# A 640-point inverse transform regrouped by residues modulo 5, with accumulating DMAs for one of its parts

## The chip, the cores and the metric

The kernel runs on one core of one Trainium2 chip. The metric is the time of one execution on the device in microseconds. A core has TensorE (PE, with its weight loads as PEld), VectorE (DVE), ScalarE (ACT), GpSimd (POOL) and SyncE (SP); each runs its own instruction queue in order. SP and POOL also issue DMAs, which 16 DMA engines carry out.

## The reference, cut to what matters

```python
xn = layernorm(x)                                   # x: 2048 x 640, bf16
X  = rfft2(xn)                                      # 2048 x 321 complex
s  = irfft2(X * (w_r + 1j * w_i)).astype(bfloat16)  # 2048 x 640
g  = silu((gelu(xn @ w_gate) * (xn @ w_up)) @ w_down)   # inner width 1536
return x + s * g
```

There are two branches, a spectral filter and a gated feed-forward network. They meet in the last line.

## The kernel before, in words

The 2048 rows are 16 slabs of 128 rows: slab n1 holds the rows that are n1 modulo 16. Four slabs make a group g of the feed-forward branch.

**Order of the work.** Everything is laid out by hand. The list `back` has 144 entries, called slots here; each slot is a piece of the feed-forward branch, and `plan[s]` holds the items of the spectral branch that `put` hangs behind slot s. The program goes through the slots in order and emits a slot's piece, then its items. Every engine sees its own instructions in that order. TensorE's queue is therefore fixed, and an engine that is late holds up whatever stands behind it in its own queue.

**Feed-forward branch.** `ffn_half(g, t, k)` is one slot: five matmuls of 128x512 into a bank `psg` (k=0, gate) or `psu` (k=1, up), both at L809. ScalarE applies gelu to psg (L814), and VectorE multiplies it by psu into `UT` (L816). The pool `psA` has two banks of each tag, so each tag has one bank ahead. Slots 96 to 107 are the down projection of group 2 and slots 108 to 131 are the 24 halves of group 3. The down projection of groups 1 and 2 is made by `product`, seven block products in place of eight for two slabs at a time: six matmuls of 320 columns each (L903), sums of its left operands by `u_sum` on VectorE (L884), and additions out of PSUM on VectorE (L910). Where the sum is complete, ScalarE takes a tanh (`th`, L847) and VectorE finishes the gate (L852), one and two products later, through `flush`. `down_third` does it directly: 12 matmuls per half slab (L946), and ScalarE applies silu to the bank (L844). In group 3, the last, slabs 12 and 13 go through `product` (slots 132 to 137) and slabs 14 and 15 through `down_third` (slots 138 to 143).

**Spectral branch.** The forward stages end with the array `B2`. From slot 67 on eleven bursts (`s2_in`, `s2_out`) do the filter: 4 to 5 matmuls into `px` (L649), ScalarE copies px to `xs` (L657), VectorE multiplies xs with the two filter tables into `RZ` (L661), and one burst later TensorE multiplies into `pu` (L674). ScalarE copies pu to `RX` (L681), the even and the odd columns apart, and SP writes RX to DRAM (`UDR`, L684). `load_V` reads it back with rows and columns exchanged (L699) into `VY` (slabs 0 to 3) and `W` (slabs 4 to 15).

The inverse transform follows, slab by slab:

- `gather` copies the columns that fill a fifth block of 128 into `vr` (VectorE, L709). Its tile has two buffers.
- `slab_S1i`, the transform over rows: five matmuls of 128x128 into `pv` (L730), one for each 128-column block of V as the weights. ScalarE copies pv to a slab of `vs` (L732).
- `group_Di`, the 640-point transform over columns, for up to three slabs at once through `d_group`: 12 matmuls of 160 columns with 128 rows (L573) and 12 with 32 rows (L577) into two tiles `pd`. ScalarE copies and scales them into `eobuf` (L755).
- `group_cs` and `group_Y`: VectorE adds and subtracts even and odd parts (L761), then writes the two halves of a row of Y, one of them backwards (L770, L772).
- `finish`: VectorE multiplies Y by the gate (L788). For slabs 0 to 11 (`XA = 12`) POOL issues a DMA that adds x out of DRAM to Y in place (L790); for the others VectorE adds x (L792). SP then writes the slab out (L793).

px, pu, pv and pd all come from the pool `psB`, which has two buffers: the third of a row of such tiles waits until the first has been copied out.

Slot 98 is called `vs0`. A group of three slabs starts every seven slots from there: S1i at +1, +2 and +4, D at +6, cs at +7 and +8, Y at +9 and +10, finish at +11 to +13.

Of the kernel before, what the change touches and what calls it, by code (L numbers as in the profile page):

```python
# [14 lines left out]
P = 128  # L15
# [61 lines left out]
def build(nc, env):  # L77
# [71 lines left out]
    FI = consts.tile([P, 5, LH], BF16)  # L149
# [91 lines left out]
    lint = gtile([LH], INT32)  # L241
    nc.gpsimd.iota(lint, pattern=[[1, LH]], base=0, channel_multiplier=0)
# [10 lines left out]
    ftm = gtile([5, LH], FP32)  # L253
# [49 lines left out]
    kc = []  # L303

    def fwd_consts():
        cq = affine("cq", h_f, -320.0, 320.0)
# [4 lines left out]
        kc.append(cq)  # L311
        ab.extend([(a_m, b_0), (a_m, b_1), (a_m, b_2), (a_m, b_3), (a_y, None)])
# [3 lines left out]
    def inv_consts(part):  # L316
        if part == 0:
            for k, c in enumerate((0.0, 4.0, 2.0)):
                inv_src[k] = affine(f"i_{k}", pf, 4.0, c)
            kc.append(affine("hk", h_f, -2.0, 1.0))  # L320
        else:
            o = [affine(f"o_{k}", pf, 2.0, c) for k, c in enumerate((320.0, 2.0, 321.0, 1.0))]
            i_0, i_1, i_2 = (inv_src[k] for k in range(3))
            ab.extend([(i_0, o[0]), (i_1, o[1]), (i_2, o[2]), (i_2, o[3])])

    def inv_rest():
        cq, hk = kc
        l_s, l_k, l_r, i_r, o_r = (c1(n) for n in ("l_s", "l_k", "l_r", "i_r", "o_r"))
        for out, in0, s1, s2 in ((l_s, s_f, 2.0, 256.0), (l_k, h_f, 2.0, l_s), (l_r, hk, hi_f, l_k),
                                 (i_r, l_r, 2.0, 0.0), (o_r, l_r, 1.0, cq)):  # L330
            nc.gpsimd.tensor_scalar(out=out, in0=in0, scalar1=s1, scalar2=s2, op0=ALU.mult, op1=ALU.add)
        ab.append((i_r, o_r))
# [28 lines left out]
    fv = gtile([10, LH], FP32)  # L361

    def ft_v(g):
        if g < 5:
            parts = [(0, TW, meo[:, g // 2])] if g < 4 else [(0, 66, mys), (66, TW, mys)]
        else:
            parts = [(0, LH, lint)]
# [4 lines left out]
    FW = (TW, LH)  # L372
# [194 lines left out]
    def d_group(lhs, T, w):  # L567
        ps = [psB.tile([P, 2, 512], FP32, tag="b", name=f"pd{b}") for b in range(2)]
        n = len(lhs)
        out = [[ps[g // 2][:, g % 2, a * w:(a + 1) * w] for g in range(4)] for a in range(n)]  # L570
        for a in range(n):
            for g in range(4):
                nc.tensor.matmul(out[a][g], lhsT=lhs[a][:, g, :], rhs=T[:, g, 0:w], start=(a == 0), stop=False)  # L573
        for a in range(n):
            for g in range(4):
                r = slice(32 * g, 32 * g + 32)
                nc.tensor.matmul(out[a][g], lhsT=lhs[a][r, 4, :], rhs=T[r, 4, 0:w], start=False, stop=(a == n - 1))  # L577
        return [t[:, :, 0:n * w].rearrange("p k (a m) -> p a k m", a=n) for t in ps]

# [50 lines left out]
    WB = LH + 1  # L630
    BURSTS = [(h0, 3, l0, w) for h0 in range(0, 15, 3) for l0, w in ((0, WB), (WB, L - WB))]
# [8 lines left out]
    def s2_in(b):  # L640
# [3 lines left out]
        for lo in range(2):  # L644
            r = slice(64 * lo, 64 * lo + 64)
            for hh in range(2):
                for i, j, kind in s2_tiles(b, lo, hh):
# [3 lines left out]
                                     stop=(j == n))  # L651

# [11 lines left out]
    def s2_out(b):  # L664
# [25 lines left out]
    VO = (0, L + 1, LH, L + 1 + HD)  # L690
# [13 lines left out]
    def gather(i):  # L704
# [3 lines left out]
        for k, c0, w in ((0, 0, LH), (1, L + 1, HD)):  # L708
# [453 lines left out]
```

## Time and profile before

| | |
|---|---|
| median of 3 runs | 196.37 us (195.82 to 196.56) |
| profiled execution | 197.07 us |
| its span | 195.2 us |
| granted TensorE clock | 1.0 |
| TensorE busy | 187.4 us, 96% |
| VectorE busy | 154.5 us, 79% |
| ScalarE busy | 126.6 us, 65% |
| POOL busy | 50.5 us, 26% |

All rows of the profile come from one execution, of 197.07 us; 1.9 us of it lie outside the span. Busy shares are means over stages: by stretches of the span, TensorE is busy for 9.55 of the 10 us from 124 to 134 and 10.98 of the 11 us from 134 to 145, and VectorE for 9.55 of those 11. A busy time of an instruction includes its start-up, which overlaps the instruction before it: a row of VectorE additions of 0.48 us each starts every 0.40 us. In a line of the timeline the idle time before the instruction and what ended it stand in brackets.

### The profile page before, as it was taken

Reading aid. Unit: us, or ns where it says so; the run is one execution under the profiler, and the core shown is the slowest. Engines: PE = TensorE matmul, PEld = TensorE weight load, DVE = VectorE, ACT = ScalarE, POOL = GpSimd, SP = SyncE. Lnnn points to the kernel's source line nnn. Section 1 sums busy time; section 2 is a strip of 40 time slices with the busy share of each in tenths; the row PEclk is TensorE's granted clock in tenths of the full one; section 3 lists DMA queues with packets and bytes.
Section 4 is the critical chain, followed back from the end, with each engine's and each line's share of the span. In section 5 each row is a group of like instructions: output and inputs, shape, how many; then the busy total and the mean of one; then the engine's idle time right before and its main releaser. Section 6 shows DMA issues by size and latency. Waiting matters only on the chain.

```text
span 195.2 us, 4162 instructions
## 1 busy us (share of the span) xinstructions
PE 187.4 (96%) x1496; PEld 115.6 (59%) x1511; DVE 154.5 (79%) x379; ACT 126.6 (65%) x224; POOL 50.5 (26%) x80
## 2 busy tenths in 40 slices
PE   7899999999999999999999999999999999999992
PEld 5788854767555566576533333456765555556772
DVE  7887888989799869899965756587888657587993
ACT  4668567866977877525697787524675757465651
POOL 4448688998030200000000000000003250404100
PEclk9999999999999999999999999999999999999999
DMA  6999999968899999269955233459400836575623
GB/s 167 302 333 358 368 306 170 152 116 259 215 157 175 196 221 230 69 169 234 172 118 116 74 101 101 115 144 288 131 3 2 164 75 150 119 143 125 136 88 85
DMA packets 39989, 32.44 MB, mean 166 GB/s; under 512 B 12960, under 2 KB 38048, under 8 KB 39840
## 3 DMA queue, kind: packets, MB, share of 16 engines
q1 hardware_dynamic: 36176, 27.91, 60.3%
q0 software_dynamic: 1824, 3.28, 10.0%
q10 hardware_dynamic: 1968, 0.98, 1.9%
q8 instruction: 12, 0.20, 0.5%
q14 instruction: 9, 0.07, 0.1%
HBM read 19.03 MB, written 7.88 MB: 138 GB/s over the span
## 4 chain that ended last, share of the span: by engine, by line
PE 80%; DMA 10%; SPq 3%; DVE 3%; ACT 2%; issue 1%; DVEq 0%; ACTq 0%
PE psu L809 25%; PE psg L809 24%; PE psg L946 5%; PE psg L903 4%; PE psu L946 4%; DMA B<-ZDR 4%; PE psu L903 3%; DMA VY<-UDR 2%; PE pz L563 2%; PE pd L573 2%; SPq L624 2%; PE pv L730 2%; PE pd L594 2%; PE pu L674 2%; DMA Tfwd<-Tinv 1%
## 5 line engine op out<-in xcount | busy, mean ns | idle before, releaser
L809 PE MATMUL psu<-XG,Wu 128*128 128x512 bf16 (+2 forms) x285 | 60.4, 342 | 0.4 <-issue 0.3
L809 PE MATMUL psg<-XG,Wg 128*128 128x512 bf16 (+2 forms) x280 | 60.0, 341 | 0.7 <-issue 0.2
L816 DVE TENSOR_TENSOR UT<-psu,ge 128x512 bf16<-128x512 f32 (+2 forms) x58 | 34.4, 594 | 15.1 <-PE psu L809 12.3
L814 ACT ACTIVATE ge<-psg 128x512 bf16<-128x512 f32 (+2 forms) x58 | 30.3, 523 | 23.2 <-PE psg L809 22.5
L809 PEld LDWEIGHTS <-Wu 128*128 128x128 bf16 x290 | 26.1, 98 | 22.5 <-issue 3.4
L809 PEld LDWEIGHTS <-Wg 128*128 128x128 bf16 x290 | 26.5, 98 | 20.2 <-issue 0.2
L790 POOL DMA_DIRECT2D VY<-in_A_x_dram x12 | 10.6, 1035 | 95.3 <-PE psu L809 74.3
L661 DVE TENSOR_TENSOR RZ<-xs,W 128x972 bf16<-128x972 bf16 (+2 forms) x22 | 13.3, 648 | 9.8 <-ACT xs L657 9.5
L903 PEld LDWEIGHTS <-UT 128*128 128x128 bf16 x150 | 14.3, 98 | 6.1 <-issue 0.2
L946 PEld LDWEIGHTS <-UT 128*128 128x128 bf16 x156 | 14.4, 98 | 5.0
L599 ACT CAST RZ<-pd 128x660 bf16<-128x660 f32 x16 | 11.3, 706 | 5.6 <-PE pd L596 5.5
L189 DVE BATCH_NORM_STATS2 st<-X 128x6 f32<-128x320 bf16 x32 | 14.0, 476 | 0.4 <-DMA X<-in_A_x_dram 0.4
L755 ACT ACTIVATE W<-pd 128x960 bf16<-128x960 f32 (+2 forms) x14 | 10.0, 778 | 5.0 <-PE pd L577 5.0
L732 ACT CAST W<-pv 128x640 bf16<-128x640 f32 x16 | 11.0, 688 | 3.3 <-PE pv L730 3.1
L681 ACT CAST RX<-pu 128x486 bf16<-128x486 f32 (+4 forms) x22 | 12.3, 560 | 0.3
L946 PE MATMUL psg<-Wd,UT 128*128 128x320 bf16 (+1 forms) x84 | 11.8, 288 | 0.0
L565 ACT CAST GEN<-pz 128x640 bf16<-128x640 f32 x16 | 11.2, 698 | 0.6 <-PE pz L563 0.6
L657 ACT CAST xs<-px 128x972 bf16<-128x972 f32 (+2 forms) x11 | 10.3, 936 | 1.6 <-PE px L649 1.4
L761 DVE TENSOR_TENSOR W<-W 128x960 bf16<-128x960 bf16 (+1 forms) x12 | 7.0, 599 | 4.3 <-ACT W L755 4.3
L946 PE MATMUL psu<-Wd,UT 128*128 128x320 bf16 (+1 forms) x72 | 10.3, 291 | 0.0
L207 POOL TENSOR_TENSOR rst<-ve,mhalf 128x1 f32<-128x1 f32 (+1 forms) x6 | 5.5, 913 | 11.6 <-DVE ve L205 11.6
L903 PE MATMUL psu<-Wd,UT 128*128 128x320 bf16 x48 | 7.8, 300 | 0.0
(207 smaller groups left out, 295.7 us busy)
## 6 DMA issues: line engine op xcount, KB each, us to landing
ZDR<-RZ SPq DMA_DIRECT2D x16, 160.5 KB, 4.5
UDR<-RX SPq DMA_DIRECT2D x10, 240.8 KB, 3.0
B<-ZDR SPq DMA_DIRECT2D x8, 240.8 KB, 5.2
W<-UDR SPq DMA_DIRECT2D x2, 963.0 KB, 9.4
X<-in_A_x_dram SPq DMA_DIRECT2D x3, 640.0 KB, 10.4
Wd<-in_B_w_down_dram SPq DMA_DIRECT2D x1, 1920.0 KB, 14.7
VY<-in_A_x_dram POOLq DMA_DIRECT2D x12, 160.0 KB, 4.0
out_dram<-VY SPq DMA_DIRECT2D x12, 160.0 KB, 3.1
```

The costliest lines, as they stand in the source:

```text
L189: nc.vector.bn_stats(out=st_n[n1][:, k, :], in_=X[:, n1, 320 * k:320 * k + 320])
L565: nc.scalar.copy(out=Zt[n1], in_=pz)
L599: nc.scalar.copy(out=zd.rearrange("p c (q e) -> p c q e", e=10), in_=pd[:, :, 0:330].rearrange("p c (e q) -> p c q e", q=33))
L661: nc.vector.tensor_tensor(out=pp[-1], in0=xs, in1=WT[:, :, h0:h0 + n, l0:l0 + w], op=ALU.mult)
L681: nc.scalar.copy(out=us[:, :, :, c0:c0 + (w + 1 - m) // 2], in_=pv[:, :, :, m:w:2])
L732: nc.scalar.copy(out=vs, in_=pv)
L790: nc.gpsimd.dma_start(out=Y, in_=xv[:, n1, sl], accum_op=ALU.add)
L809: nc.tensor.matmul(ps, lhsT=WT[:, c, t * P:(t + 1) * P], rhs=xnT[g][:, c, c0:c1_], start=(c == 0), stop=(c == 4))
L814: nc.scalar.activation(out=ges[t], in_=ps, func=ACT.Gelu_apprx_tanh)
L816: nc.vector.tensor_tensor(out=UT[:, t, c0:c1_], in0=ps, in1=ges[t], op=ALU.mult)
L903: nc.tensor.matmul(ps, lhsT=lhs[:, t, :], rhs=rhs[:, t, :], start=(t == 0), stop=(t == 5))
L946: nc.tensor.matmul(ph, lhsT=UT[:, t, j * P:(j + 1) * P], rhs=Wd[:, t, c0:c1_], start=(t == 0), stop=(t == NT - 1))
```

## The change

The columns of the inverse transform are sorted by their residue modulo 5 (and parity) in place of parity alone.

- **Bursts.** The bursts split a row of 321 at column 160 in place of 162. `s2_sort` replaces the two copies of pu: VectorE copies residues 1 and 3 modulo 10 ahead of its multiplications, and in each second burst one last column; ScalarE copies five residues and then three.
- **D stage.** `slab_Di` does the column transform slab by slab: five matmuls of 128x128, each with its own weights, into one pd tile, and one ScalarE copy of 640. Four of the five blocks go through cs and Y, which now write the first 128 and, backwards, the last 128 columns of each half row of 320, where they wrote 160 and 160. `group_rest` gets the 64 columns between them as minus a sum of the written ones (two VectorE sums, one ScalarE copy), and the fifth block, which has period 128 over the row, is added to all five 128-column blocks of Y: for slabs 0 to 8 (`YA = 9`) by one accumulating DMA per slab on POOL's queue, from `eobuf` to Y with the source block repeated five times, for the others by VectorE.
- **Slabs 12 and 13** go through `down_third`, with no `product` and no `u_sum` for group 3.
- **Places.** A group of three slabs starts every six slots from slot 98: S1i at +2, +3 and +5, D at +4, +6 and +7, cs at +8, Y at +9, the two rest sums at +10, ScalarE's copy at +12, the addition of the fifth block at +13, finish at +17 to +19 (slabs 0 to 8) or +15 to +17. The gathers for slabs 4 to 7, 8 to 11 and 12 to 15 move from slots 104, 113 and 122 to 103, 111 and 120.
- Tables and constants of the inverse transform follow: `FI` is 128 wide, not 161.

The core of the diff; the bodies of `d_group`, `quad`, `group_Di`, `group_cs` and `group_Y` that go out are printed above:

```diff
-    FI = consts.tile([P, 5, LH], BF16)
+    FI = consts.tile([P, 5, P], BF16)
...
-    WB = LH + 1
-    BURSTS = [(h0, 3, l0, w) for h0 in range(0, 15, 3) for l0, w in ((0, WB), (WB, L - WB))]
+    WB = LH
+    BURSTS = [(h0, 3, l0, w) for h0 in range(0, 15, 3) for l0, w in ((0, HD), (HD, WB))]
...
+        return px
+    def s2_mul(b, px):
+        h0, n, l0, w = BURSTS[b]
...
+        return pu
+    def s2_sort(b, pu, part):
+        h0, n, l0, w = BURSTS[b]
         ut = st_b["u"][:, (h0 // 3 + 1) % 2, 0:2 * n, :]
         us = ut.rearrange("p (h k) l -> p k h l", k=2)
         pv = pu[:, :, 0:n * w].rearrange("p k (h l) -> p k h l", l=w)
-        for m in range(2):
-            c0 = m * LH + l0 // 2
-            nc.scalar.copy(out=us[:, :, :, c0:c0 + (w + 1 - m) // 2], in_=pv[:, :, :, m:w:2])
-        if l0 + w == L:
-            for lo in range(2):
-                nc.sync.dma_start(out=rows(UDR, lo, h0, h0 + n), in_=turned(ut, lo, 0, n))
+        m, nq = l0 // 10, w // 10
+        for r0, ni, c0, copy in (((1, 2, HD + 97, nc.vector.tensor_copy),),
+                                 ((0, 5, P, nc.scalar.copy), (5, 3, HD + 1, nc.scalar.copy)))[part]:
+            step = -32 if r0 == 0 else 32
+            out = bass.AP(us.tensor, us.offset + c0 + m, [list(us.ap[d]) for d in (0, 2, 1)] + [[step, ni], [1, nq]])
+            src = bass.AP(pv.tensor, pv.offset + r0, [list(pv.ap[d]) for d in (0, 2, 1)] + [[2, ni], [10, nq]])
+            copy(out=out, in_=src)
+        if l0 + w < L:
+            return
+        if part == 0:
+            nc.vector.tensor_copy(out=us[:, :, :, HD:HD + 1], in_=pv[:, :, :, w - 1:w])
+            return
+        for lo in range(2):
+            nc.sync.dma_start(out=rows(UDR, lo, h0, h0 + n), in_=turned(ut, lo, 0, n))
+    def s2_step(b):
+        px = s2_in(b) if b < len(BURSTS) else None
+        pu = s2_out(b - 1) if b else None
+        if b:
+            s2_sort(b - 1, pu, 0)
+        if px is not None:
+            s2_mul(b, px)
+        if b:
+            s2_sort(b - 1, pu, 1)
     st_c = {}
     VP = ((0, 2), (2, 2), (4, 4), (8, 4), (12, 4))
     VA = 4
-    VO = (0, L + 1, LH, L + 1 + HD)
+    VO = (0, L, HD + 33, L + HD + 33)
     def load_V():
         VY = big.tile([P, NH * L], BF16, tag="sB", name="VY")
...
-        for k, c0, w in ((0, 0, LH), (1, L + 1, HD)):
-            nc.vector.tensor_copy(out=vr.rearrange("p n (b k i) -> p n b k i", b=2, k=2)[:, :, :, k, :],
-                                  in_=V[:, :, c0:c0 + 2 * w].rearrange("p n (b c) -> p n b c", b=2)[:, :, :, P:HD])
+        nc.vector.tensor_copy(out=vr[:, :, 0:64].rearrange("p n (b i) -> p n b i", b=2),
+                              in_=V[:, :, P:P + 66].rearrange("p n (b i) -> p n b i", b=2)[:, :, :, 0:32])
+        nc.vector.tensor_copy(out=vr[:, :, 64:P], in_=V[:, :, L + P + 1:L + P + 65])
+    YA = 9
...
+    eobuf = w1f[:, 4 * D:10 * D].rearrange("p (s x) -> p s x", s=2)
+    csbuf = w1f[:, 10 * D:10 * D + 6 * 512].rearrange("p (s x) -> p s x", s=2)
+    ubuf = w1f[:, 10 * D + 6 * 512:10 * D + 6 * 512 + 3 * 256]
+    def parts(buf, i, g):
         n = DG[i][1]
+        return buf[:, i % 2, 0:g * n * P].rearrange("p (g a n) -> p g a n", g=g, a=n)
+    def halves(i):
+        return st_c["Y"](*DG[i]).rearrange("p a (h n) -> p a h n", h=2)
+    def slab_Di(n1):
+        i = n1 // 3
+        vs = st_c.pop(n1)
+        pd = psB.tile([P, 5, P], FP32, tag="b", name="pd")
+        for g in range(5):
+            nc.tensor.matmul(pd[:, g, :], lhsT=vs[:, g, :], rhs=FI[:, g, :], start=True, stop=True)
+        nc.scalar.activation(out=parts(eobuf, i, 5)[:, :, n1 - DG[i][0], :], in_=pd, func=ACT.Copy,
+                             scale=(2.0 if n1 // 4 in BY_SILU else 1.0) / (S * D))
+    def group_cs(i, q):
+        eo, cs = parts(eobuf, i, 5), parts(csbuf, i, 4)
+        nc.vector.tensor_tensor(out=cs[:, 2 * q:2 * q + 2], in0=eo[:, 0:2], in1=eo[:, 2:4],
+                                op=(ALU.add, ALU.subtract)[q])
+    def group_Y(i, q):
+        cs = parts(csbuf, i, 4)
+        Y = halves(i)
+        C, Z = (cs[:, k:4:2].rearrange("p h a n -> p a h n") for k in range(2))
+        if q == 0:
+            nc.vector.tensor_tensor(out=Y[:, :, :, 0:P], in0=C, in1=Z, op=ALU.add)
+        else:
+            nc.vector.tensor_tensor(out=Y[:, :, ::-1, 319:191:-1], in0=C, in1=Z, op=ALU.subtract)
+    def group_rest(i, q):
         n0, n = DG[i]
+        Y = halves(i)
+        u = ubuf[:, 0:n * 256].rearrange("p (a h b e) -> p a h b e", h=2, b=2, e=64)
         if q == 0:
+            Yb = Y.rearrange("p a h (b e) -> p (a h) b e", e=64)
+            nc.vector.tensor_tensor(out=u.rearrange("p a h b e -> p (a h) b e"), in0=Yb[:, :, 0:2], in1=Yb[:, :, 4:2:-1],
+                                    op=ALU.add)
+        elif q == 1:
+            nc.vector.tensor_tensor(out=u[:, :, 0], in0=u[:, :, 0], in1=u[:, :, 1, ::-1], op=ALU.add)
+        elif q == 2:
+            nc.scalar.activation(out=Y[:, :, :, P:P + 64], in_=u[:, :, 0], func=ACT.Copy, scale=-1.0)
         else:
+            Yt = st_c["Y"](n0, n).rearrange("p a (t e) -> p a t e", t=5)
+            Yp = parts(eobuf, i, 5)[:, 4].unsqueeze(2).to_broadcast([P, n, 5, P])
+            if n0 < YA:
+                for a in range(n):
+                    nc.gpsimd.dma_start(out=Yt[:, a], in_=Yp[:, a], accum_op=ALU.add)
+            else:
+                nc.vector.tensor_tensor(out=Yt, in0=Yt, in1=Yp, op=ALU.add)
...
-        if a == 0 and i in (1, 2, 3) and g in STR:
+        if a == 0 and i in (1, 2, 3):
...
-        if g == 3:
-            for k in range(6):
-                back.append((run,) + tuple((product, g, 0, i) for i in range(k * 7 // 6, (k + 1) * 7 // 6)))
-        for j in range(2 if g == 3 else 0, 4):
+        for j in range(4):
...
-    for g, at in ((1, 56), (2, 92), (3, 128)):
+    for g, at in ((1, 56), (2, 92)):
-        if g in STR:
-            put(at + 1, u_sum, nc.vector, g, 1, 0, TB)
+        put(at + 1, u_sum, nc.vector, g, 1, 0, TB)
...
     sb = 67
     AT = (0, 3, 5, 7, 9, 11, 13, 15, 17, 19, 21)
     for b in range(len(BURSTS)):
-        put(sb + AT[b], s2_in, b)
-        if b > 0:
-            put(sb + AT[b], s2_out, b - 1)
-    put(sb + 23, s2_out, len(BURSTS) - 1)
+        put(sb + AT[b], s2_step, b)
+    put(sb + 23, s2_step, len(BURSTS))
     sb += 24
     put(sb, load_V)
     vs0 = sb + 7
-    for i, at in enumerate((vs0 - 1, vs0, vs0 + 6, vs0 + 15, vs0 + 24)):
+    LAST = len(back) - 1
+    for i, at in enumerate((vs0 - 1, vs0, vs0 + 5, vs0 + 13, vs0 + 22)):
         put(at, gather, i)
     for pair in range(XA // 2, 8):
         put(vs0 + 4 * pair, load_xt, pair)
     for i, (n0, n) in enumerate(DG):
-        a = vs0 + 7 * i
+        a = vs0 + 6 * i
         for k in range(n):
-            put(a + ((1, 2, 4)[k] if n == 3 else 1), slab_S1i, n0 + k)
-        d = a + 6 if n == 3 else a + 4
-        put(d, group_Di, i)
-        for q in range(2):
-            put(d + 1 + (q if n == 3 else 0), group_cs, i, q)
-        for q in range(2):
-            put(d + (3 + q if n == 3 else 1), group_Y, i, q)
+            put(a + (2, 3, 5)[k], slab_S1i, n0 + k)
+            put(a + (4, 6, 7)[k], slab_Di, n0 + k)
+        d = a + (7 if n == 3 else 4)
+        for k, it in enumerate(((group_cs, 0), (group_cs, 1), (group_Y, 0), (group_Y, 1), (group_rest, 0),
+                                (group_rest, 1), (group_rest, 2), (group_rest, 3))):
+            put(min(d + (1, 1, 2, 2, 3, 3, 5, 6)[k], LAST), it[0], i, it[1])
         for k in range(n):
-            put(min(d + (5 + k if n == 3 else 2), vs0 + 41), finish, n0 + k)
+            put(min(d + (10 if n0 < YA else 8) + k, LAST), finish, n0 + k)
```

More of the change, by code (lines that the diff above doesn't have):

```diff
@@ L252, in build @@
     scr = goff[0]
-    ftm = gtile([5, LH], FP32)
+    ftm = gtile([5, TW], FP32)
     vt = gtile([NS, P], INT32)
@@ L316, in inv_consts @@
     def inv_consts(part):
[L317 to L324, printed above, removed]
+        for name, a, b in ((("x_e", -4.0, 8.0), ("x_o", -6.0, 7.0)),
+                           (("x_t", 10.0, 0.0), ("x_w", -10.0, 5.0), ("x_b", -320.0, 320.0)))[part]:
+            inv_src[name] = affine(name, hi_f, a, b)
     def inv_rest():
[L327 to L330, printed above, removed]
+        x = inv_src
+        y_e, y_o, y_m, k_e, k_o, k_m = (c1(n) for n in ("y_e", "y_o", "y_m", "k_e", "k_o", "k_m"))
+        for out, in0, s1, s2 in ((y_e, h_f, -2.0, x["x_e"]), (y_o, h_f, 2.0, x["x_o"]), (y_m, h_f, x["x_w"], x["x_t"]),
+                                 (k_e, s_f, 10.0, y_e), (k_o, s_f, 10.0, y_o), (k_m, s_f, 10.0, y_m)):
             nc.gpsimd.tensor_scalar(out=out, in0=in0, scalar1=s1, scalar2=s2, op0=ALU.mult, op1=ALU.add)
-        ab.append((i_r, o_r))
+        ab.extend([(k_e, b_0), (k_e, b_1), (k_o, b_0), (k_o, b_1), (k_m, x["x_b"])])
     fwd_consts()
@@ L565, in slab_S1 @@
         nc.scalar.copy(out=Zt[n1], in_=pz)
[L567 to L578, printed above, removed]
     DG = [(n0, min(3, NS - n0)) for n0 in range(0, NS, 3)]
```

39 lines of the change are left out of this document (6 added, 33 removed).

## The prediction

> **What bounds the kernel now.** I read the engine table first, then TensorE's own waits, then the chain of waits, and last the timeline from slot 96 on, where the change lies.
>
> ```profile
> PE 187.4 (96%) x1496; PEld 115.6 (59%) x1511; DVE 154.5 (79%) x379; ACT 126.6 (65%) x224; POOL 50.5 (26%) x80
> ```
>
> TensorE is busy for 187.4 of 195.2 us, and its listed waits sum to 3.6 us, most of them at the start. So the time is TensorE's program; the other engines count only where they are late enough to hold a PSUM buffer that TensorE wants next. The chain of waits says what the touched pieces cost (start, us, what):
>
> ```profile
> 139.67 0.85 PE pd L573 x12
> 140.52 0.32 PE pd L577 x12
> 140.84 0.92 PE psg L903 x6
> 141.76 0.82 PE psu L903 x6
> ...
> 182.90 0.81 PE psu L903 x6
> 183.71 0.82 PE psg L903 x6
> 184.53 0.28 PE pd L573 x4
> 184.81 0.18 PE pd L577 x4
> ...
> 188.36 1.63 PE psg L946 x12
> ```
>
> A D group of three slabs costs 0.85 + 0.32 = 1.17 us, and the matmuls after it take 0.92 in place of 0.81; a block product costs 0.815; twelve direct matmuls of 320 columns cost 1.63. The timeline (start, us, engine, line, wait in brackets) has the price of five matmuls of 128x128 and the one real wait of this part:
>
> ```profile
> 133.59 0.34 PE L730 MATMUL pv<-Tinv,VY 128*128 128x128 bf16 x3 [0.34 <-DMA VY<-UDR]
> 133.64 0.30 DVE L709 COPY vr<-VY 128x128 bf16<-128x128 bf16 x2 [0.94 <-DMA VY<-UDR]
> ...
> 140.85 0.36 DVE L709 COPY vr<-W 128x256 bf16<-128x256 bf16 x2 [0.32 <-DMA W<-UDR]
> ...
> 142.41 0.39 PE L730 MATMUL pv<-Tinv,VY 128*128 128x128 bf16 x4
> 142.63 0.22 PE L730 MATMUL pv<-Tinv,vr 128*128 128x128 bf16 x1
> 142.69 0.98 PE L903 MATMUL psg<-Wd,UT 128*128 128x320 bf16 x6
> ```
>
> From 142.41 to 142.69, one S1i slab takes TensorE 0.28 us. The first S1i slab starts at 133.03 and the next product at 134.06: 1.03 us, so 0.75 are a wait for UDR's way back.
>
> **The change, part by part.** TensorE first.
>
> 1. D stage. Out go five groups at 1.17 and slab 15 at 0.28 + 0.18: 6.31 us. In come 16 slabs of five 128x128 matmuls, each with its own weights, the form of the S1i row: 16 x 0.28 = 4.48. Gain 1.83. The slow start after each group (0.92 against 0.81, and 1.74 against 1.63 after slab 15) goes too, since S1i leaves none: 6 x 0.11 = 0.66. I take 0.6.
> 2. Slabs 12 and 13. Out go 7 products x 0.815 = 5.71. In come 48 direct matmuls at 1.63/12 = 0.136: 6.52. Cost 0.81. VectorE loses seven u_sums (about 2.7 us) and seven PSUM additions (0.4 each, start to start), which TensorE did not wait for.
> 3. S1i moves from slot 99 to slot 100, behind one more product (0.82): of the wait of 0.75 about 0.08 stays. Gain 0.67, if UDR lands when it did.
>
> TensorE alone: -1.83 - 0.6 + 0.81 - 0.67 = -2.3 us. Now what the other engines may take back.
>
> 4. Bursts. ScalarE loses two copies of about 0.58 and gets two of 480 and 288 elements: its rows (640 in 0.69, 320 in 0.43) give 0.57 and 0.41. VectorE gets a PSUM copy of 192 elements ahead of the two multiplications. Its 320-element row takes 0.48, so 0.35; in every second burst a copy of six elements, at most 0.17 more. The copy runs while ScalarE still does xs: by the row at 103.02, px ends near 103.4, pu at 103.8, VectorE would be done at 104.2 to 104.4, and xs ends at 104.57. So nothing is late in the steady bursts. In the first two, VectorE has no idle time (90.3 to 97.6): I put 0.2 us of loss there. Bounds: 0 and 0.35 x 2.
> 5. Slots 100 to 107. Every slot now takes one buffer of psB (two in all), so a ScalarE eviction must end within one slot. ScalarE's queue there also has the th activations, which wait for VectorE's additions, and VectorE is busy without a break from 133.64 to 139.9. The eviction of S1i slab 1 now stands behind the th of products 4 and 5, the later of which ran at 137.28; it ends near 138.4. TensorE wants that buffer near 138.0: 0.4 us lost. The gather for slabs 4 to 7 moves from slot 104 to 103 and meets the same landing (140.85): VectorE waits 0.9 instead of 0.3, and products 9 to 11, queued behind it, are added 0.4 later; their banks are wanted only two products of the same tag later, so that costs TensorE nothing.
> 6. Slots 108 to 131. Six slots take 6 x 1.08 + 6 x 0.28 = 8.2 us. ScalarE works three gelus (0.6), six evictions (0.6 start to start) and one copy of 384 (0.49), 5.9 us in all; VectorE three multiplications, two cs and two Y of 768, two rest sums, three finishes and half a gather, about 7. Both fit. I allow 0.4 for the odd late buffer.
> 7. Accumulating DMAs: nine more on POOL, three per group, on a queue that now issues three per group. First the timeline's two kinds of issue on POOL, then the queue table's lines of POOL's and ScalarE's queue (packets, MB, share), then the source view of L790:
>
> ```profile
> 67.07 1.39 POOL L128 DMA_DIRECT2D W<-W  x2 [11.62 <-DMA XG<-X]
> 149.60 2.74 POOL L790 DMA_DIRECT2D VY<-in_A_x_dram  x3 [74.28 <-PE psu L809]
> ```
>
> ```profile
> q0 software_dynamic: 1824, 3.28, 10.0%
> q10 hardware_dynamic: 1968, 0.98, 1.9%
> ```
>
> ```profile
> DMA to landing us min/median/max: 3.3/4.0/5.0
> ```
>
> The source repeats a 128-column block five times, so each transfer has 640 pieces of 256 B where L790 has 128 of 1280 B. Moving: queue 0 holds 16 engines for 10% of 195.2 us over 14 transfers, 1.4 us each; landing then stays at 4.0 us if bytes decide and goes to 4.0 + 4 x 1.4 = 9.6 if pieces do. The nearest row for small pieces is q10's (1968 packets of 500 B in 1.9% of 16 engines, 30 ns each): 40 pieces per engine at 30 to 60 ns are 1.2 to 2.4 us in place of 1.4, so I take 4 to 5. Issuing: 0.9 us (L790) if pieces do not count, 4.5 if they count in full. L128 takes 0.70 with some 144 packets (1824 less 12 x 128, over two), L790 0.9 with 128, so the count does not set their order; I stay near the low end, 1 to 1.7.
>
> Who waits: VectorE's finish for those slabs, four slots (5.4 us) after the issue, and ScalarE's eviction of the D slab two groups on, which overwrites the source buffer: slab 6 (slot 114) waits for the transfer of slab 0 (issued at slot 111), slabs 7 and 8 (116, 117) for the next two. With TensorE's end of slot 110 as zero, gelu and ScalarE's copy end at 1.2, the first transfer with an issue of g lands at 1.3 + g + 3.1, and the eviction in slot 114 is due at 4 x 1.36 + 0.28 + 0.4 = 6.1: free up to g = 1.7, with one slot of slack behind that. POOL needs 3g + 3 x 0.9 in the 8.2 us of a group: free up to g = 1.8. So I charge nothing.
>
> On the issue the Trainium skill ("DMA: Bandwidth & Descriptors", Anatomy of one DMA — SWDGE path) says that descriptor generation is a small share and that many can be emitted before the cost shows; by that the sum stays as it is. The same page's Specifications speak against the change: below 512 B a transfer works by read-modify-write; its section on small descriptors limits that to HBM, and these stay in SBUF. No row here shows either.
>
> 8. Early part: the inverse table is 128 wide in place of 161 and its constants are fewer; POOL and ScalarE save some tenths off the path. Nothing.
>
> The tail keeps its last three thirds and its 3.5 us behind TensorE: the chain from the last matmul on is untouched, and VectorE's added rest sums (1.1 us for three slabs) end five slots ahead of it.
>
> Sum: -2.3 + 0.2 + 0.4 + 0.4 = -1.3 us. The profiled execution took 197.07 us (span 195.2 and 1.9 around it), which is 0.7 above the median of the runs. 197.07 - 1.3 = 195.8 profiled, 195.1 as a median.
>
> **The rivals.**
>
> The issue of 256 B pieces is slow (slower). Above g = 1.8 POOL falls behind by 3(g - 1.8) per group, over three groups, with about 1.5 us of slack: at 2.5 us +5, less the 1.3 gained, 199 to 200; at 3 us 204; at 4.5 over 215. A landing of 9.6 us would come to the same as g near 3. For it: no row shows an issue with so many pieces, and the accumulating issue is the dearer one with fewer packets. Against it: L128 moves four times the bytes of L790 in a shorter issue. 0.22.
>
> The gain goes into slots 100 to 131 (no change). VectorE is at its limit in the product slots and rest sums are added right behind them; if it is some 2 us late, ScalarE's copy in slot 110 waits for it, the evictions behind that wait, and TensorE loses a slot's slack in the first two groups: about 1 us more, 196.1. For it: window 134 to 145 has VectorE at 9.55 of 11 us. Against: it recovered there with the larger D group. 0.13.
>
> The sorting copy is slow (slower). Its reads step through PSUM by ten. pu waits for the multiplication, which ends 0.38 us early (105.86 against 106.24). If the copy takes 1 us, each of ten steps loses 0.2 to 0.3: 197.4. Against: ScalarE's copy at L599 reads PSUM with a stride of 33 and keeps its rate (0.706 us for 660 elements, 0.688 for 640 at L732). 0.07.
>
> TensorE gains nothing, since a weight load of 98 ns sets the pace of the 128-column matmuls: 16 x 5 x 0.098 = 7.8 us, 3.3 more than in 1, 198.4. The S1i rows deny it. 0.03.
>
> **How the numbers follow.** The forecast has 0.55: 195.1, between 194.1 (the whole -2.3) and 195.9 (twice the losses). A measurement of this kernel tells about 0.5%, 1 us. Faster than 195.4 is some 0.78 of the forecast case: 0.43. Within 0.5%: the rest of it, nearly all of the second rival and part of the third: 0.26. Slower: 0.31, the first rival, the fourth and most of the third. The range goes from 194.0 to 199.5; outside lie the upper half of the slow issue and a gain above -2.3, below 0.2 together.
>
> **What would show it.** L573 and L577 become one line with five matmuls in 0.28 us and no slow start behind them; TensorE's wait for VY is gone; POOL's row for VY<-W stays under 1.8 us; ScalarE's evictions of pd show no wait for a DMA; VectorE's finishes wait for none either. Wrong would be POOL busy without a break from 148 on, or TensorE waiting for ScalarE at pv and pd in more than two slots.

## The result and the profile after

| | before | after |
|---|---|---|
| median of 4 runs each, same chip | 196.12 us (195.82 to 196.56) | 201.41 us (200.56 to 201.79) |
| profiled execution | 197.07 us | 201.79 us |
| its span | 195.2 us | 200.0 us |

The ratio is 1.0244 (95% interval 1.0202 to 1.0285): the changed kernel is 2.4% slower, where 195.1 us, 0.6% faster than 196.37, had been predicted. 201.41 also lies above the range. The ratio is an estimate over the runs of the batch; the plain quotient of the two medians, 1.027, lies inside its interval. Medians below are over all executions, and the ratios leave out two slow ones, 201.31 us of e2 and 1113.43 us of e8.

The waits of the profile after, by engine and line, from 129 us on (total us, how often, longest):

```profile
ACT W L764 <- DMA VY<-W: 8.1, 2, 5.0
DVE VY L816 <- DMA VY<-W: 7.4, 5, 3.4
...
PE pd L763 <- ACT W L764: 5.4, 2, 3.6
```

L764 is ScalarE's eviction of a D slab, L816 VectorE's multiplication in finish, L763 the D matmuls. The prediction named the first two as the waits that would show it wrong, and the third is what they do to TensorE: it lacks a buffer of psB twice. The queue table's line of POOL's queue after (packets, MB, share of 16 engines):

```profile
q0 software_dynamic: 7728, 4.76, 17.7%
```

and what the source view of L798, the nine new DMAs, says of their landing:

```profile
DMA to landing us min/median/max: 4.5/7.0/8.7
```

7728 less the 1824 of before for nine transfers are 656 each. The transfers land in 7.0 us at the median, where the prediction took 4 to 5. The timeline of POOL after has the order in which that does harm (start, us, what, idle before):

```profile
158.22 0.84 POOL L818 DMA_DIRECT2D VY<-in_A_x_dram  x1 [0.96 <-DVE VY L816]
158.75 4.87 POOL L798 DMA_DIRECT2D VY<-W  x3
...
168.89 0.84 POOL L818 DMA_DIRECT2D VY<-in_A_x_dram  x1 [0.41 <-DVE VY L816]
169.43 4.88 POOL L798 DMA_DIRECT2D VY<-W  x3
```

The first three, from 148.84 on, are issued in 4.63 us, 1.54 each, as predicted (1 to 1.7). But ahead of each group's fifth blocks in POOL's queue stands the x of the last slab of the group before. ScalarE's timeline shows the copy that the second group's fifth blocks need (L792) done at 156.41 and that of the third at 166.72; POOL issued them at 158.75 and 169.43, 2.3 and 2.7 us late, each time right behind an x (L818). And then ScalarE and TensorE, from the timeline after:

```profile
176.49 0.70 ACT L764 ACTIVATE W<-pd 128x640 bf16<-128x640 f32 x1 [4.97 <-DMA VY<-W]
...
177.24 0.69 PE L763 MATMUL pd<-FI,W 128*128 128x128 bf16 x5 [3.65 <-ACT W L764]
```

The first of the third group's transfers lands at 176.4; only then may ScalarE overwrite the source buffer with slab 12, and TensorE, which has been without a buffer for 3.65 us, goes on. The chain of waits after has the same way in one piece, from an x over two groups of transfers to that eviction:

```profile
158.22 0.84 POOL VY L818
159.06 1.45 POOL VY L798
160.51 7.57 DMA VY<-W
...
168.90 0.54 POOL VY L818
169.43 6.97 DMA VY<-W
...
176.49 0.71 ACT W L764
```

The gain is there too. The chain of waits where S1i and the new D stage begin:

```profile
133.02 0.81 PE psg L931 x6
133.83 0.28 PE pv L736 x5
...
136.83 0.28 PE pd L763 x5
137.11 0.81 PE psg L931 x6
```

D costs 0.28 us a slab, a product behind it 0.81 instead of 0.92, S1i no longer waits, and nothing waits around slots 100 to 107.

### The profile page after: what moved, and what is told of

Its sections match the earlier page's. It is cut to its first block, busy times and chain, and to the rows that moved or that the text cites. A ratio compares the mean times of both kernels' runs of the same rounds, so it can differ in the third digit from the quotient of the medians.

```text
span 200.0 us, 4117 instructions
## 1 busy us (share of the span) xinstructions
PE 188.1 (94%) x1453; PEld 116.7 (58%) x1469; DVE 158.2 (79%) x391; ACT 127.3 (64%) x231; POOL 63.7 (32%) x90
## 3 DMA queue, kind: packets, MB, share of 16 engines
q0 software_dynamic: 7728, 4.76, 17.7%
q10 hardware_dynamic: 1968, 0.98, 1.8%
## 4 chain that ended last, share of the span: by engine, by line
PE 86%; DMA 7%; POOL 2%; ACT 1%; DVE 1%; issue 1%; POOLq 0%; DVEq 0%; ACTq 0%
PE psu L837 24%; PE psg L837 22%; DMA VY<-W 7%; PE psg L974 7%; PE psu L974 6%; PE psu L931 6%; PE psg L931 6%; PE pu L657 2%; PE psg L588 2%; PE pz L555 2%; PE pd L573 2%; PE pd L763 2%; PE px L628 2%; PE pv L736 1%; POOL VY L818 1%
## 5 line engine op out<-in xcount | busy, mean ns | idle before, releaser
L798 POOL DMA_DIRECT2D VY<-W x9 | 14.4, 2373 | 77.8 <-ACT W L764 77.8
L764 ACT ACTIVATE W<-pd 128x640 bf16<-128x640 f32 x16 | 11.3, 704 | 11.9 <-DMA VY<-W 8.1
L644 DVE TENSOR_TENSOR RZ<-xs,W 128x960 bf16<-128x960 bf16 (+2 forms) x22 | 13.3, 647 | 3.0 <-ACT xs L640 2.7
L974 PE MATMUL psg<-Wd,UT 128*128 128x320 bf16 (+1 forms) x108 | 15.5, 290 | 0.0
L818 POOL DMA_DIRECT2D VY<-in_A_x_dram x12 | 10.3, 886 | 15.1 <-DVE VY L816 11.0
L974 PE MATMUL psu<-Wd,UT 128*128 128x320 bf16 (+1 forms) x96 | 13.9, 292 | 0.0
L763 PE MATMUL pd<-FI,W 128*128 128x128 bf16 x80 | 7.6, 229 | 5.4 <-ACT W L764 5.4
L672 ACT CAST RX<-pu 128x480 bf16<-128x480 f32 (+3 forms) x22 | 10.8, 490 | 2.2 <-DVE RX L672 1.2
L816 DVE TENSOR_TENSOR VY<-VY,XG 128x640 bf16<-128x640 bf16 x12 | 5.8, 488 | 7.4 <-DMA VY<-W 7.4
L763 PEld LDWEIGHTS <-W 128*128 128x128 bf16 x80 | 6.2, 103 | 9.2 <-issue 6.3
L640 ACT CAST xs<-px 128x960 bf16<-128x960 f32 (+2 forms) x11 | 10.3, 934 | 1.6 <-PE px L628 1.4
```

Of the source, the lines that this page charges most:

```text
L644: nc.vector.tensor_tensor(out=pp[-1], in0=xs, in1=WT[:, :, h0:h0 + n, l0:l0 + w], op=ALU.mult)
L763: nc.tensor.matmul(pd[:, g, :], lhsT=vs[:, g, :], rhs=FI[:, g, :], start=True, stop=True)
L764: nc.scalar.activation(out=parts(eobuf, i, 5)[:, :, n1 - DG[i][0], :], in_=pd, func=ACT.Copy, scale=(2.0 if n1 // 4 in BY_SILU else 1.0) / ...
L798: nc.gpsimd.dma_start(out=Yt[:, a], in_=Yp[:, a], accum_op=ALU.add)
L818: nc.gpsimd.dma_start(out=Y, in_=xv[:, n1, sl], accum_op=ALU.add)
L974: nc.tensor.matmul(ph, lhsT=UT[:, t, j * P:(j + 1) * P], rhs=Wd[:, t, c0:c1_], start=(t == 0), stop=(t == NT - 1))
```

## The experiments

The theory after the result: a chain from group to group. The landing of a group's transfers holds back VectorE's finish; that holds back the x of the group's last slab; POOL's queue puts the next group's transfers behind it; and a late landing then holds ScalarE's eviction two groups on. The rivals: the transfers cost time one by one (short pieces, addition, crowded DMA engines); the reuse of the source buffer alone is the cause; or the rest of the change (VectorE's new sums, slabs 12 and 13) costs the time. The first four runs tested the length of the transfers; the chain stands in the expectations from e5 on. There "theory 1" is the length of the transfers (short pieces, full DMA engines), "theory 2" a slow addition inside SBUF whatever the pieces, and "theory 3", later "the loop", the chain. All ratios are against the kernel before on the same chip in the same batch (medians 196.12 for the changed kernel, then 196.20 for e1 to e4, 196.49 for e5 to e8 and 196.36 for e9 to e11).

| run | median us | ratio (interval) | landing, median us | TensorE waits for ScalarE at pd, us |
|---|---|---|---|---|
| changed kernel | 201.41 | 1.0244 (1.0202 to 1.0285) | 7.0 | 5.4 |
| e1_vector_add | 194.76 | 0.9925 (0.9906 to 0.9944) | none | 0 |
| e2_long_rows | 198.14 | 1.0089 (1.0047 to 1.0131) | 5.1 | 3.2 |
| e3_third_buffer | 202.87 | 1.0341 (1.0305 to 1.0377) | 7.0 | 0 |
| e4_no_x | 194.75 | 0.9928 (0.9905 to 0.9952) | 5.8 | 0 |
| e5_pool_ahead | 198.72 | 1.0090 (1.0053 to 1.0127) | 7.6 | 2.9 |
| e6_finish_later | 196.58 | 0.9997 (0.9976 to 1.0018) | 5.0 | 0.5 |
| e7_products_back | 198.95 | 1.0112 (1.0083 to 1.0141) | none | 0 |
| e8_direct_alone | 196.96 | 1.0013 (0.9986 to 1.0039) | none | 0 |
| e9_no_add | 197.62 | 1.0104 (1.0032 to 1.0176) | 4.6 | 2.1 |
| e10_ahead_later | 196.51 | 1.0014 (0.9983 to 1.0045) | 5.1 | 1.3 |
| e11_one_group | 194.80 | 0.9924 (0.9902 to 0.9946) | 5.0 | 0 |

**e1_vector_add.** VectorE adds the fifth block for all slabs; finish then comes two slots earlier, as the changed kernel has it for slabs 9 to 15.

```diff
-    YA = 9
+    YA = 0
```

> All theories: with no accumulating DMA for the fifth block no eviction and no finish waits for one, so TensorE's 5.4 us of waits for ScalarE and the slow clock after them go. What is left is the TensorE gain alone, 2 us below the kernel before: 194.0 to 194.6. Rival: VectorE, which gets 1.1 us more in each of the first three groups of 8.2 us and then has about 8.1 us of work in them, becomes late and holds psu or ScalarE's copy: 195.5 to 197.

194.76 us, just above the expected 194.6 and 6.65 us less than the changed kernel: against the kernel before (196.20 in this batch) that is the whole loss of 5.2 us and 1.4 us more. The rest of the change is a gain; the nine DMAs are the cause, at a price of 6.65 us. The engine table of this run:

```profile
PE 186.6 (97%) x1453; PEld 116.2 (60%) x1469; DVE 160.4 (83%) x394; ACT 127.4 (66%) x231; POOL 50.1 (26%) x81
```

TensorE waits for no buffer from 129 us on. Its last matmuls end at 189.41 against 191.66 before, 2.25 us earlier. By medians the gain is 1.4 us (1.1 to 1.8): the profiled execution of before, 197.07 us, lay 0.9 above the median of this batch. The DMAs had taken three additions of 1.15 us off VectorE, which was not late anyway. This version beats both kernels.

**e2_long_rows.** The same number of bytes to the same place, but each partition's source is one run of 640 elements and not a block of 128 read five times; for four fifths of the columns another block is added.

```diff
-        return buf[:, i % 2, 0:g * n * P].rearrange("p (g a n) -> p g a n", g=g, a=n)
+        t = buf[:, i % 2, 0:g * n * P]
+        if g == 5:
+            return t.rearrange("p (a g n) -> p g a n", g=g, a=n)
+        return t.rearrange("p (g a n) -> p g a n", g=g, a=n)
...
-                    nc.gpsimd.dma_start(out=Yt[:, a], in_=Yp[:, a], accum_op=ALU.add)
+                    nc.gpsimd.dma_start(out=st_c["Y"](n0 + a, 1)[:, 0, :], in_=eobuf[:, i % 2, a * D:a * D + D],
+                                        accum_op=ALU.add)
```

> The source of each accumulating DMA is 640 neighbouring columns of the same slab, so it has 128 pieces of 1280 B; waits and bytes are the same (the wrong block is added for four fifths of the columns). Theory 1, the 256 B pieces keep the DMA engines busy: packets on queue 0 fall from 7728 to about 3000, the issue from 1.6 to 0.9 us, landing from 7.0 to 4 to 5 us, ScalarE's wait of 8.1 us to under 1, time 194 to 196. Theory 2, an accumulating transfer inside SBUF is slow whatever its pieces: landing stays near 7 us, time near 201.

198.14 us, half of the 6.65 us gone and between the two expected ranges. Queue 0 has 3120 packets in 13.8% of 196.3 us, so 144 a transfer. Against e1's 1824 packets in 8.8% of 193.0 us that is (0.138 x 196.3 - 0.088 x 193.0) / 9 = 1.1 us of each engine per transfer; in the changed kernel (0.177 x 200.0 - 0.088 x 193.0) / 9 = 2.0. An issue falls from 1.54 to 0.90 us and the landing from 7.0 to 5.1. So the pieces matter; but e2 is still 3.4 us above e1, and POOL still issues the second and third group right behind an x, at 158.82 and 168.08.

**e3_third_buffer.** A third source buffer, in the space of RZ, so that no eviction meets a transfer of two groups before.

```diff
+    eo3 = RZ.rearrange("p b l -> p (b l)")[:, 0:3 * D]
...
+        if g == 5:
+            t = eo3 if i % 3 == 2 else buf[:, i % 3, :]
+            return t[:, 0:g * n * P].rearrange("p (g a n) -> p g a n", g=g, a=n)
```

> eobuf gets a third buffer, so ScalarE's eviction of pd waits for the transfer of three groups back; the transfers and VectorE's finishes are as in the changed kernel. If ScalarE's wait is what stops TensorE: its wait for pd goes from 5.4 us to under 1, landing stays at 6 to 9 us, VectorE still waits some 7 us in finish, time 195 to 197. If VectorE's wait takes its place (finish ahead of the multiplications that free psu, and ahead of the sums that ScalarE's copy needs): TensorE waits 2 to 4 us elsewhere, 198 to 200.

202.87 us, no better, and above both expected ranges. ScalarE's wait for the DMA is gone and the wait turns up elsewhere. The waits of this run:

```profile
DVE VY L821 <- DMA VY<-RZ: 5.6, 3, 3.8
PE psg L979 <- DVE UT L849: 5.4, 2, 2.9
```

VectorE's finish waits 5.6 us for landings out of the third buffer and 3.8 for the others, with the multiplications into UT (L849) queued behind it, and `down_third` (L979) needs UT: TensorE stands for the same 5.4 us at another place. The source buffer is where the lateness first shows and not its cause.

**e4_no_x.** POOL adds no x for slabs 0 to 11.

```diff
-        if n1 < XA:
-            nc.gpsimd.dma_start(out=Y, in_=xv[:, n1, sl], accum_op=ALU.add)
-        else:
+        if n1 >= XA:
```

> Leaves out the addition of x for slabs 0 to 11, so POOL issues only the nine transfers of the fifth block. Theory 1 in its stronger form, the 16 DMA engines are full (three transfers of the fifth block, three of x and three to the output in 8.2 us): landing of the fifth block falls from 7.0 to about 5 us and the time to 196 to 198. If the transfers are slow by themselves or by each other: landing stays at 6.5 to 7, time 200 to 201.

194.75 us, below both expected ranges and as fast as without the nine DMAs, though these are all there, 656 packets each. POOL's timeline in this run, second and third group:

```profile
156.95 4.50 POOL L798 DMA_DIRECT2D VY<-W  x3 [3.23 <-ACT VY L792]
165.10 4.54 POOL L798 DMA_DIRECT2D VY<-W  x3 [3.65 <-ACT VY L792]
```

Each group is issued when ScalarE's copy is done and lands in 5.8 us at the median. This run takes away two things, x in POOL's queue and x on the DMA engines; the next two keep x and change the order.

**e5_pool_ahead.** The fifth blocks are issued one slot earlier.

```diff
-            put(min(d + (1, 1, 2, 2, 3, 3, 5, 6)[k], LAST), it[0], i, it[1])
+            put(min(d + (1, 1, 2, 2, 3, 3, 5, 5 if n0 < YA else 6)[k], LAST), it[0], i, it[1])
```

> The fifth-block transfers of a group stand one slot earlier in POOL's queue, ahead of the x transfer of the third slab of the group before, which waits for VectorE's finish, which waits for the last of that group's fifth-block transfers. Theory 3, this loop is most of the damage (the transfers of the second group started at 158.75 though ScalarE's copy ended at 156.4, those of the third at 169.43 against 166.7): they start 1.5 to 2.5 us earlier, ScalarE's wait falls from 8.1 us to 2 or 3, TensorE's from 5.4 to under 1, time 195 to 197. Theory 1, the length of the transfers alone: the waits move by as little as the start, the landing grows with the overlap, time 199 to 201.

198.72 us, between the expected ranges, and the landing does not fall (7.6). The fifth blocks now go ahead of the x of slab 2, but stay behind that of slab 1, which waits for the same landings: the third group is issued at 166.94, 1.4 us after ScalarE's copy instead of 2.7. The chain is loosened and still closed: 2.7 of the 6.65 us are gone, by a change of order on POOL's queue alone.

**e6_finish_later.** The finishes of slabs 0 to 8 come three slots later.

```diff
-            put(min(d + (10 if n0 < YA else 8) + k, LAST), finish, n0 + k)
+            put(min(d + (13 if n0 < YA else 8) + k, LAST), finish, n0 + k)
```

> The finishes of slabs 0 to 8 come three slots (4.1 us) later, so VectorE should not wait for a transfer of 7 us, and the x transfers come behind the next group's fifth-block transfers on POOL. Theory 3: VectorE's and POOL's waits for transfers go to under 1 us, landing goes to 5 to 6, TensorE's waits vanish, time 194.3 to 195.3. Theory 1: landing stays at 7 us because of the pieces, ScalarE still waits for 1 to 3 us per group, time 196 to 199.

196.58 us, with every transfer in place. All x of a group now stand behind the next group's fifth blocks. POOL's timeline in this run:

```profile
156.96 4.50 POOL L798 DMA_DIRECT2D VY<-W  x3 [3.12 <-ACT VY L792]
159.59 4.55 POOL L818 DMA_DIRECT2D VY<-in_A_x_dram  x3
165.11 4.54 POOL L798 DMA_DIRECT2D VY<-W  x3 [0.96 <-ACT VY L792]
```

The issue times are those of e4, although the DMA engines have as much to do as in the changed kernel (a share of 0.99 from 149 to 182 us against 1.00), and TensorE waits 0.5 us instead of 5.4. The share adds up packets that are under way side by side: from 174.5 to 175 us of the changed kernel it is 1.57, so 1.00 does not mean full. So a change of order alone takes away 4.8 of the 6.65 us. The time lies in the range expected from the length of the transfers (196 to 199), but the landing, 5.0 us, and the issue times are those expected from the chain. The edit moves the finishes on VectorE's queue as well as the x on POOL's; how much of the 4.8 us belongs to each queue is not shown. The other 1.8 against e1 show in two places: TensorE's last matmul ends at 190.06 against 189.41, and from the last VectorE operation to the end of the span it takes 3.6 us against 2.8, where five x and 15 of the 20 pieces of the output go out after 178 us, eight of these between 188.3 and 191.6 (in e1 two x and 11 pieces after 178 us). That the crowding makes the end longer was not tried by itself.

**e7_products_back.** e1 with the block products of slabs 12 and 13 restored.

```diff
+        if g == 3:
+            for k in range(6):
+                back.append((run,) + tuple((product, g, 0, i) for i in range(k * 7 // 6, (k + 1) * 7 // 6)))
-        for j in range(4):
+        for j in range(2 if g == 3 else 0, 4):
...
-    for g, at in ((1, 56), (2, 92)):
+    for g, at in ((1, 56), (2, 92), (3, 128)):
```

The parts not shown set `YA` to 0 and give the sums for group 3 their place and their calls again.

> The kernel with the fifth block added by VectorE (194.76 us), with slabs 12 and 13 through block products again. By the prediction's term 2 TensorE needs 0.8 us less: 193.9 to 194.2. If VectorE, which gets the sums and PSUM additions back (about 6 us) beside the rest sums and two additions of 1.15 us, holds TensorE or the end: 195 to 196.5.

198.95 us, 4.2 more than e1 and above both expected ranges. The view by windows has VectorE, the third pair of columns, busy for 9.90 of 10 us, and the waits have TensorE held by VectorE's addition out of PSUM (L938):

```profile
175.00:185.00 10.00, 8.45 (x61) 5.42 (x60) 9.90 (x24) 4.83 (x8) 2.59 (x3) 1.00 0.77 167
```

```profile
PE psg L974 <- DVE Tfwd L938: 2.2, 1, 2.2
```

The direct products, which cost TensorE time (e8), are what makes room on VectorE for the new sums.

**e8_direct_alone.** The kernel before with slabs 12 and 13 through `down_third` and nothing else: the same lines the other way round.

```diff
-        if g == 3:
-            for k in range(6):
-                back.append((run,) + tuple((product, g, 0, i) for i in range(k * 7 // 6, (k + 1) * 7 // 6)))
-        for j in range(2 if g == 3 else 0, 4):
+        for j in range(4):
...
-    for g, at in ((1, 56), (2, 92), (3, 128)):
+    for g, at in ((1, 56), (2, 92)):
```

> The kernel before with only slabs 12 and 13 changed to direct matmuls. Term 2 by itself: 0.8 us slower, 196.9 to 197.2. If VectorE's relief is worth as much as TensorE's longer program: no change, 196.2.

Ratio 1.0013 (0.9986 to 1.0039): between a gain of 0.3 us and a loss of 0.8. TensorE's end is 191.84 against 191.66, but this execution began slot 96 earlier, at 129.23 against 129.77; counted from there, TensorE's program is 0.72 us longer.

**e9_no_add.** The nine transfers write instead of adding.

```diff
-                    nc.gpsimd.dma_start(out=Yt[:, a], in_=Yp[:, a], accum_op=ALU.add)
+                    nc.gpsimd.dma_start(out=Yt[:, a], in_=Yp[:, a])
```

> The nine fifth-block transfers only write instead of adding (the fifth block replaces the sum of the other four, for slabs 0 to 8); size, pieces of 256 B, order and waits are those of the changed kernel. Theory A, the 640 short pieces hold the DMA engines whether or not something is added: each transfer still takes about 2.0 us of every engine, the landing stays at 4.5 / 7.0 / 8.7 us, ScalarE and VectorE still wait some 8 and 7 us for it, and the time is 200 to 202 us. Theory B, adding is what costs (the destination has to be read as well): each transfer takes 1.0 to 1.3 us of every engine, as pieces of 30 ns in the SyncE queue do (40 per engine), the landing falls to 3 to 5 us, and the time to 195.5 to 198 us.

197.62 us, inside the range of theory B. This was meant to separate the addition from the short pieces and does not, since without the addition the same transfer is no longer cut up. The queue table:

```profile
q0 software_dynamic: 2400, 4.76, 11.7%
```

That is (2400 - 1824) / 9 = 64 packets a transfer instead of 656, 0.66 us of each engine, an issue of 0.90 us and a landing of 4.6. (The pieces of 30 ns in the expectation are those of ScalarE's queue, q10.) What the addition costs at equal pieces stays open. The run shows something else: with a third of the engine time the loss against e1 is still 2.9 us. POOL issues the second and third group at 159.22 and 167.97, again right behind an x.

**e10_ahead_later.** e5 and e6 together.

```diff
-            put(min(d + (1, 1, 2, 2, 3, 3, 5, 6)[k], LAST), it[0], i, it[1])
+            put(min(d + (1, 1, 2, 2, 3, 3, 5, 5 if n0 < YA else 6)[k], LAST), it[0], i, it[1])
...
-            put(min(d + (10 if n0 < YA else 8) + k, LAST), finish, n0 + k)
+            put(min(d + (13 if n0 < YA else 8) + k, LAST), finish, n0 + k)
```

> Both moves of the two earlier runs in one: the fifth-block transfers are issued one slot earlier, ahead of the x of the group before, and the finishes of slabs 0 to 8 come three slots later. Theory of a loop over GpSimd's queue (a fifth-block transfer behind an x that waits for a finish that waits for the landing of the group before): the later finish alone has opened it already, since its transfers went out right behind ScalarE's copy, at 156.96 and 165.11; the earlier slot then changes nothing, 196 to 197 us. Theory of time in slots alone (each move gives the transfers so much more time to land): the moves add up, ScalarE's wait of 2.6 us goes, and the time is 195.5 us or less.

196.51 us, that of e6, as expected from the chain. (The waits in the table come from its profiled execution, at 198.26 us the slowest of ten.) Once the order is open, the earlier slot brings nothing: the gains do not add up, as those of more time to land would.

**e11_one_group.** Only slabs 0 to 2 by DMA.

```diff
-    YA = 9
+    YA = 3
```

> Only slabs 0 to 2 get their fifth block by DMA; VectorE adds those of slabs 3 to 15. Theory of a loop from group to group: one group has no group before it, its transfers go out at 149 to 152 and land within 5 us, no evictions or finishes wait for more than 1 us, and the time is that of the kernel with VectorE alone, 194.5 to 195.2 us. Rival, each transfer costs by itself (the 6.6 us between the changed kernel and the one with VectorE alone are 0.74 for each of nine): three cost 2.2 us, about 197 us.

194.80 us, that of e1, as expected from the chain. Three transfers of 656 packets, issued at 149.27 and landing in 5.0 us, cost nothing that can be measured, and nobody waits for them. The price is not paid transfer by transfer; it needs a second group behind the first.

Together: the whole loss takes long transfers, an x ahead of them in POOL's queue and several groups. Without x (e4) or with one group alone (e11) none of it is left. Opening the order (e6) takes away most of it with the transfers as long as they are; shortening them (e2, e9) takes away 3.3 and 3.8 of the 6.65 us with the order as it is. The two parts act on each other, so they cannot be added.

## Why the prediction was wrong, point by point

- **TensorE's program (terms 1 to 3, -2.3 us): right.** From the first product of slot 96 to TensorE's end it takes 61.89 us before (129.77 to 191.66) and 59.69 in e1 (129.72 to 189.41), 2.2 less, with D at 0.28 a slab, no slow start, and no wait before S1i. Direct products for slabs 12 and 13 were put at 0.81 more; e8 measures -0.3 to +0.8 by its ratio and 0.72 by its rows. That VectorE's lost work was nothing TensorE waited for holds for the kernel before alone: with the new sums it is worth 4.2 us (e7), which the prediction did not see, and which did no harm to the sum because both came together.
- **Allowances (terms 4 to 6, 1.0 us): the first right, the others not needed.** From the first matmul into px to the first product of slot 96 the bursts take 39.87 us before (89.90 to 129.77) and 40.12 in e1 (89.60 to 129.72): 0.25 more, where 0.2 was put. VectorE's sorting copy of 192 elements took 0.35 us, as worked out, and in each second burst the six elements 0.17. No wait shows in slots 100 to 107, and e1 has none behind them, so nothing was seen of the 0.8 us of terms 5 and 6. With terms 1 to 3 that makes about -1.9 us between two single executions; the medians say -1.4 (-1.8 to -1.1). That the latter is close to the forecast sum of -1.3 does not make terms 5 and 6 right.
- **Accumulating DMAs (term 7, charged nothing): the step that failed.** It had the waiters right, the issue right (1.54 us) and the condition right for the first group, whose source buffer is free in time (landing 5.0 us at the median, no wait at slots 114 to 117). Its estimate of 1.2 to 2.4 us of each DMA engine holds too (2.0, worked out at e2). Two of its steps failed. The landing was taken as 4 to 5 us and was 7.2 in the second and third groups. The bound of 9.6 us "if pieces do" was left to a rival, as all or nothing, where the truth lies between. And POOL was costed as a sum, "3g + 3x0.9 in the 8.2 us of a group", which was satisfied: from 155 to 175 POOL is busy 7.16 of 10 us. What decides is the order inside the queue. The x of slab 2 stands ahead of the next group's fifth blocks and waits, through VectorE, for the landing of this group's; no step asked what the moved instructions wait for in turn. One reading of rows was wrong as well: the changed kernel less e4 gives (7728 - 6000) / 12 = 144 packets for an x and not 128, so each transfer of L128 has (1824 - 12 x 144) / 2 = 48 and not 144. Issues of 0.70, 0.9 and 1.54 us then belong to 48, 144 and 656 packets: their order goes with the count. The row for L128 was no evidence against a dear issue, and that 1.54 us still fell inside 1 to 1.7 was in part luck. The 1.4 us "each" likewise was the mean of unlike transfers; an x takes (0.177 x 200.0 - 0.114 x 193.0) / 12 = 1.1 us of each engine.
- **The sum of the profiled executions.** After minus before is 4.7 us: -2.25 of gain, +5.4 of waits, and the slow clock behind the longer wait, (0.69 - 0.28) + (2.13 - 1.08) + (0.48 - 0.28) = 1.7 in the chain of waits. That makes 4.8.
- **The rivals.** The first came true in its second form, a long landing, at a price between its own (199 to 204 us), though the issue itself was not slow. The range ended at 199.5, since the upper half of this rival was left outside it. The second fell with e1, the third with the sorting copy, and the fourth with D at 0.28.
- **The skill's sentences.** The Trainium skill ("DMA: Bandwidth & Descriptors", Why small descriptors are slow) limits the penalty of short pieces to HBM. Here source and destination both lie in SBUF, the additions are part of the transfer, and the short pieces still cost 2.0 us of each engine against 1.1 (e2). For these accumulating transfers the measurement decides. The same page's Anatomy of one DMA — SWDGE path has descriptor generation as a small share; an issue took 1.54 us with 656 packets and 0.90 with 144, so the dependence is weak for such a count, but it is there.

## What to carry to other kernels

A queue with spare time can still close a circle: for every DMA that an edit adds to an in-order queue, ask what the instruction ahead of it waits for, and follow that back until it either ends or arrives at the added DMA of the round before. A landing time that depends on unknown pieces is a range, and the condition "free up to" should be worked out for the landing as well as for the issue. Work taken off an engine that is not late buys nothing, and a cheap VectorE addition (1.15 us for three slabs) can be better than a DMA that ties three queues together.

## What the runs showed of the hardware

- The clock after a wait. View by windows of the changed kernel, the stretch behind the wait of 3.65 us; the column ahead of the last two is the granted clock:

```profile
177.00:180.00 3.00, 2.76 (x12) 1.38 (x12) 0.49 (x1) 2.28 (x5) 1.75 (x2) 0.50 1.08 216
```

  Five matmuls of 512 columns take 2.13 us there instead of 1.08. After the wait of 1.77 us the clock stayed at 1.00, and so it did in e5 after one of 2.94. The length alone does not decide: in e3 a wait of 2.55 us, behind a stretch in which TensorE was busy, was enough. The granted clock is 1.00 there up to 179.5 us and 0.50 from 180.0, before the one matmul that ends the wait at 180.18, and that matmul, of 320 columns, takes 0.45 us. The Trainium skill ("TensorE: Matmul & The Clock Gate", Why this matters for your kernels) asks for no idle gaps above some 3 us between bursts; the waits of 3.65, 2.94 and 1.77 us agree, the one of 2.55 us in e3 does not, and there the measurement decides. Why it differs is open.
- The same 160 KB are 656, 144 or 64 packets: added from a repeated block, added from one run, written from a repeated block. They took 2.0, 1.1 and 0.66 us of each DMA engine. The first group alone, before any other transfer of that queue moves, gives the same: 2.1 (69.4% of 9 us for 1968 packets), 1.1 (39.9% of 8 us for 432) and 0.7 (25.9% of 8 us for 192). Their issues took 1.54, 0.90 and 0.90 us.
